# Moving the second layer's bias to ScalarE, running its last 64 features in pairs on two row tiles, and dropping PE's waits on itself

## The chip, the cores and the metric

The kernel runs on one core of a Trainium2 chip. The metric is the device time of one execution in microseconds (us). Each kernel was run four to six times, and the kernel before beside it; the ratios use runs in the fast state, and every profile shown fell in that state, with a granted TensorE clock of 1.0. Lines such as L735 are lines of the kernel's source. PE is TensorE's matmul, PEld its weight load, ACT is ScalarE, DVE is VectorE. PSUM holds the sums of the matmuls, here in eight banks; to evict a bank is to copy its result out. A matmul on a row tile uses 64 of the 128 rows of TensorE's array (shape 64\*128 in the profile), one on a column tile 64 of its 128 columns (128\*64).

## The reference, cut to what matters

```python
g = sigmoid((x * gate_w).sum(-1, keepdims=True))
a = A(x)        # a state-space model: B projection, recurrence over time, C projection
h = gelu(x @ w1 + b1)            # x: 2048 tokens x 640, w1: 640 x 1728
b = h @ w2 + b2                  # w2: 1728 x 640
out = g * a + (1 - g) * b
```

The inner width is 1728 = 13 x 128 + 64. A contraction over it takes 13 full slices of 128 rows and one of 64. This last, half-empty slice is what the change is about.

## The kernel before: the parts that matter

The kernel is a list of operations with priorities. A small scheduler in Python orders them for each engine, and each operation waits on the semaphores of the operations that it depends on:

```python
def run(eg, deps=deps, eng=eng, fn=fn):
    E.wait(eng, *[d.done for d in deps])        # also where PE depends on PE
    return fn()
```

The tokens are 16 chunks of 128. For each chunk the second layer makes two outputs of 128 x 320, one for each half of the 640 columns, each in a PSUM bank of its own. The banks rotate through all eight. The last slice has 64 features and, as row 65, a row of ones against which the weights hold the bias:

```python
def m2(c):                                       # second layer, chunk c
    q, t4 = c // 4, c % 4
    for hf in range(2):
        bank = next_bank()
        ...
        for jf in range(NF):                     # NF = 14 slices
            n = 128 if jf < NF - 1 else FL + 1   # the last: 64 features and the ones
            t = nc.tensor.matmul(PS[bank][:, 0:HALF],
                                 Gl[q % 2][0:n, jf, t4 * 128:(t4 + 1) * 128], W2sb[0:n, jf, cols],
                                 start=(jf == 0), stop=(jf == NF - 1))
        ...                                      # then ScalarE evicts the bank, times 1 - g

def outs(q):
    for c in range(4 * q, 4 * q + 4):
        m2(c); cproj(c); comb(c)                 # cproj: the C projection, 20 matmuls of 320 columns
```

The first layer has the same odd slice on its output side. It was already run as pairs, on two *column* tiles (`m1_tail`, two blocks of tokens at a time, 10 matmuls). This gives a model for what the change does.

Of the kernel before, what the change touches and what calls it, by code (L numbers as in the profile page):

```python
# [9 lines left out]
BF16 = mybir.dt.bfloat16  # L10
I32 = mybir.dt.int32
ACT = mybir.ActivationFunctionType
# [135 lines left out]
class Prog:  # L148
# [8 lines left out]
    def op(self, name, eng, dur, reads, writes, fn, prio=None, lat=0.0, after=()):  # L157
        deps = {}
        for k in reads:
            for w in self.last_w.get(k, ()):  # L160
                deps[w.idx] = w
        for k in writes:
            for w in self.last_w.get(k, ()):
                deps[w.idx] = w
            for r in self.last_r.get(k, ()):
                deps[r.idx] = r
        for a in after:
            deps[a.idx] = a
        deps = list(deps.values())
        E = self.E  # L170

        def run(eg, deps=deps, eng=eng, fn=fn):
            E.wait(eng, *[d.done for d in deps])
            return fn()

        it = self.sch.add(name, eng, dur, deps, run, prio=prio, lat=lat)
        for k in writes:
            self.last_w[k] = [it]
            self.last_r[k] = []
        for k in reads:  # L180
            self.last_r.setdefault(k, []).append(it)
        return it


def bass_gated_mix__ssm_conv_s5__dense_activation_gelu__prompt_kernel(
# [18 lines left out]
    _, S, D = A_x.shape  # L204
    P = A_Lambda_re.shape[0]
    F = B_w1.shape[1]
    assert S % 512 == 0 and D % 128 == 0 and P == D
    KD = D // 128
    KP = P // 128
    NQ = S // 512  # L210
    NCH = S // 128
    T = 256
    NB = S // T
    NF = (F + 127) // 128
    FL = F - (NF - 1) * 128
    assert FL <= 64
    HALF = D // 2
# [8 lines left out]
    with ExitStack() as es:  # L226

        def SB(name, shape, dt):
            return es.enter_context(nc.sbuf_tensor(name, list(shape), dt))

        xT = [SB(f"xT_{i}", [128, KD, 512], BF16) for i in range(NQ)]
        xn = [SB(f"xn_{i}", [128, 4, D], BF16) for i in range(2)]
        W1sb = SB("W1sb", [128, KD, F], BF16)
        W2sb = SB("W2sb", [128, NF, D], BF16)
        BT = SB("BT", [128, 2, KD, P], BF16)
        CT = SB("CT", [128, 2, KP, D], BF16)
        Gl = [SB(f"Gl_{i}", [128, NF, 512], BF16) for i in range(2)]
        dsk = SB("dsk", [128, D], BF16)
        gwb = SB("gwb", [128, D], BF16)
        rows = SB("rows", [128, 128], BF16)  # L240
        cols = SB("cols", [128, 3 * KP + NF], FP32)
        lcol = cols[:, 0:3 * KP].rearrange("p (a k) -> p a k", a=3)
        b1col = cols[:, 3 * KP:3 * KP + NF]
# [42 lines left out]
        PS = [es.enter_context(nc.psum_tensor(f"ps{i}", [128, 512], FP32)) for i in range(8)]  # L286
# [10 lines left out]
        E = Emitter(nc, engines, sems)  # L297
        E.count = dict.fromkeys(sems, 0)
        pr = Prog(E)
        op = pr.op  # L300

        def inc(eng, ins):
            return E.inc(eng, ins, eng + "_s")
# [8 lines left out]
        def d_act(n):  # L312
            return 0.26 + n * 0.00084
# [4 lines left out]
        def d_mm(n):  # L318
            return n / 2400.0 + 0.004


        def load(name, eng, sem, dst, src, writes, prio, dur=0.5, lat=2.5, reads=(), **kw):
            def fn():
                return dma_inc(eng, engines[eng].dma_start(dst, src), sem)
            return op(name, eng, dur, reads, writes, fn, prio=prio, lat=lat)
# [16 lines left out]
        nmain = (NF - 1) * 128  # L342
# [58 lines left out]

        op("warm", "pe", 3.2, ["wz"], [("bank", 6)], f_warm, prio=-1000)

        def f_ones():
            inc("dve", nc.vector.memset(Gl[0][64:65, NF - 1, :], 1.0))
            return inc("dve", nc.vector.memset(Gl[1][64:65, NF - 1, :], 1.0))

        op("ones", "dve", 1.1, (), ["gl1"], f_ones, prio=-40)

        XT = {q: [("xT", q, k) for k in range(KD)] for q in range(NQ)}  # L410

        psC = PS[7][:, :].bitcast(BF16)[:, 0:128]
# [140 lines left out]
        xnload(0, "sp", prio=32.4)  # L553
        load("w2a", "sp", "l_w2a", W2sb[:, 0:NF - 1, :], B_w2[0:nmain, :].rearrange("(j p) d -> p j d", p=128), ["w2a"], prio=33, lat=8.0)
        load("w2b", "sp", "l_w2b", W2sb[0:FL, NF - 1, :], B_w2[nmain:F, :], ["w2b"], prio=34, lat=4.0)
        for ci, src in enumerate((A_C_re, A_C_im)):
            load_T(f"C{ci}", f"l_C{ci}", [(CT[:, ci, :, :], src)], [("CT", ci)], prio=36 + ci, dur=4.1)
        load("dsk", "sp", "l_dsk", dsk[:, :], A_Dskip.partition_broadcast(128), ["dsk"], prio=38)
# [6 lines left out]
        def pe_prio():  # L565
            ctr["pe"] += 1
            return ctr["pe"]


        def next_bank():  # L570
            ctr["bank"] += 1
            return (ctr["bank"] - 1) % 8
# [21 lines left out]
        def m1_first():  # L594
            seq = [(k, jf) for k in range(KD) for jf in range(NW)]
            seq.remove((0, NW - 1))
            seq.insert(seq.index((1, NW - 1)), (0, NW - 1))
            for k, jf in seq:

                def f_mm(jf=jf, k=k):  # L600
                    return inc("pe", nc.tensor.matmul(PS[jf][:, :], W1sb[:, k, jf * 128:(jf + 1) * 128], xT[0][:, k, :],  # L601
                                                      start=(k == 0), stop=(k == KD - 1)))

                op(f"m1_0_{jf}_{k}", "pe", d_mm(512), [("xT", 0, k), ("w1", k)], [("bank", jf)] + (["late"] if (k, jf) == (KD - 1, 0) else []),
                   f_mm, prio=pe_prio())
            for jf in range(NW):
                ctr["bank"] += 1

                def f_ge(jf=jf):
                    return inc("act", nc.scalar.activation(Gl[0][:, jf, :], PS[jf][:, :], ACT.Gelu_apprx_tanh, bias=b1col[:, jf:jf + 1]))  # L610

                op(f"ge_0_{jf}", "act", d_act(512), [("bank", jf), "b1col"], [("gl", 0, jf)], f_ge, prio=10)
# [19 lines left out]
        def m1_tail(q):  # L632
            bank = next_bank()

            def f_mm():
                t = None
                for k in range(KD):
                    for i in range(2):
                        t = nc.tensor.matmul(PS[bank][64 * i:64 * i + FL, :], W1sb[:, k, nmain:F], xT[q + i][:, k, :],  # L639
                                             start=(k == 0), stop=(k == KD - 1))  # L640
                return inc("pe", t)

            op(f"m1t_{q}", "pe", KD * d_mm(512) + 0.25, XT[q] + XT[q + 1] + [("w1", "r")], [("bank", bank)], f_mm, prio=pe_prio())
            for i in range(2):

                def f_ge(i=i):
                    return inc("act", nc.scalar.activation(Gl[i][0:FL, NF - 1, :], PS[bank][64 * i:64 * i + FL, :], ACT.Gelu_apprx_tanh,
                                                           bias=b1col[64 * i:64 * i + FL, NF - 1:NF]))

                op(f"get_{q}_{i}", "act", d_act(512), [("bank", bank), "b1col"], [("gl", i, NF - 1)], f_ge, prio=10)  # L650

        def bproj(q):
            for ci in range(2):
# [68 lines left out]
            op(f"post{b}", "dve", 2 * d_dve(2560, 2) + 2 * d_dve(1280, 2), ["W", "ptab"], ["V", ("H", b % NHB)], f_post, prio=102 + 10 * b)  # L722


        def m2(c):
            q, t4 = c // 4, c % 4
            for hf in range(2):
                bank = next_bank()
                cols = slice(hf * HALF, (hf + 1) * HALF)

                def f_mm(bank=bank, cols=cols):
                    t = None
                    for jf in range(NF):
                        n = 128 if jf < NF - 1 else FL + 1
                        t = nc.tensor.matmul(PS[bank][:, 0:HALF], Gl[q % 2][0:n, jf, t4 * 128:(t4 + 1) * 128], W2sb[0:n, jf, cols],  # L735
                                             start=(jf == 0), stop=(jf == NF - 1))
                    return inc("pe", t)

                op(f"m2_{c}_{hf}", "pe", NF * d_mm(HALF), [("gl", q % 2, jf) for jf in range(NF)] + ["gl1", "w2a", "w2b", "b2"],
                   [("bank", bank)], f_mm, prio=pe_prio())  # L740

                def f_ev(bank=bank, cols=cols):
                    return inc("act", nc.scalar.activation(E1[c % NE][:, cols], PS[bank][:, 0:HALF], ACT.Copy, scale=g1col[:, c:c + 1]))  # L743

                op(f"e1_{c}_{hf}", "act", d_act(HALF), [("bank", bank), ("g", q)], [("E1", c % NE, hf)], f_ev, prio=5)


        cbank = {}

# [66 lines left out]

            op(f"st{c}", "sp", 0.5, [("osb", c % NO, 0), ("osb", c % NO, 1)], [], f_st, prio=1000 + c, lat=2.5)

        def outs(q):
            for c in range(4 * q, 4 * q + 4):  # L820
                m2(c)
                cproj(c)
                comb(c)

        m1_first()
        load("b2", "pool", "l_b2", W2sb[64:65, NF - 1, :], B_b2.rearrange("(o n) -> o n", o=1), ["b2"], prio=-30, dur=1.0, reads=["late"])

        m1(0, NW)
        bproj(0)
        ssm(0)  # L830
        gates(0)
        m1(1)
        m1_tail(0)
        ssm(1)
        bproj(1)
        ssm(2)
        gates(1)
        outs(0)
        for q in range(2, NQ):
            ssm(2 * q - 1)  # L840
            bproj(q)
            ssm(2 * q)
            m1(q)
            if q % 2 == 1:
                m1_tail(q - 1)
            xnload(q, "pool")
            gates(q)
            outs(q - 1)
        ssm(2 * NQ - 1)
        outs(NQ - 1)  # L850

        order = pr.sch.order()
        ptr = {e: 0 for e in order}
# [57 lines left out]
```

## Time and profile before

| | before |
|---|---|
| time, median of 3 (later 4) runs | 216.51 us |
| span of the profiled execution | 215.1 us |
| PE / DVE / ACT busy | 98% / 88% / 46% |
| second-layer matmuls | 448, of which 32 have 65 rows |

The busy line of the page (engine, busy us, share of the span, number of instruction records; POOL is GpSimd):

```profile
PE 210.9 (98%) x1247; PEld 122.0 (57%) x1257; DVE 189.3 (88%) x262; ACT 99.0 (46%) x169; POOL 3.0 (1%) x11
```

The chain of work that ended last, in order of time (start us, length us, what); L735 is the second layer, L762 the C projection, L639 the first layer's tail, L660 the B projection, and "issue" is time in which the engine waited for nothing that the profile shows:

```profile
45.30 1.22 PE ps L639 x10
46.52 0.14 issue
46.66 10.74 PE ps L660 x49
57.40 3.81 PE ps L735 x28
61.21 2.72 PE ps L762 x20
63.93 3.81 PE ps L735 x28
67.74 2.72 PE ps L762 x20
...
```

TensorE is the limit, and it does not stop: 28 matmuls of 320 columns take 3.81 us, 136 ns each, and the next group follows at once. In such a stream only a change in the number or the spacing of matmuls moves the time.

The groups by shape (line, engine, operation, out<-in, shapes, count, then busy us and mean ns, then idle before):

```profile
L735 PE MATMUL ps<-W2sb,Gl 128*128 128x320 bf16 x416 | 61.4, 299 | 0.0
L735 PE MATMUL ps<-W2sb,Gl 65*128 65x320 bf16 x32 | 9.6, 301 | 0.0
L639 PE MATMUL ps<-xT,W1sb 128*64 128x512 bf16 x20 | 2.5, 384 | 0.0
...
L743 ACT ACTIVATE E<-ps,g1col 128x320 bf16<-128x320 f32 x32 | 16.9, 527 | 43.8 <-PE ps L735 43.8
L647 ACT ACTIVATE Gl<-ps,cols 64x512 bf16<-64x512 f32 x4 | 2.7, 683 | 1.1 <-PE ps L639 1.0
```

A matmul of 65 rows lasts as long as one of 128 (301 and 299 ns; these are latencies, and the next one starts 136 ns later). The 20 tail matmuls of L639 are busy for 2.5 us in all, because they run two at a time.

### The profile page before, as it was taken

The numbers are of one execution on the slowest core, as the hardware profiler recorded it, in microseconds if no ns is written. First come the engines' busy times: TensorE is split into PE (matmuls) and PEld (weight loads), VectorE is DVE, ScalarE is ACT, GpSimd is POOL, SyncE is SP. The second block draws the span as 40 slices with busy tenths as digits, with TensorE's granted clock in tenths as the row PEclk, the third lists the DMA queues.
The fourth block names the chain that finished last, engine by engine and source line by source line (L and its number), as shares of the span: only waits on it lengthen the run. The fifth ranks groups of instructions, "written<-read, shape, count | busy, mean of one in ns | idle before, by whom it ended". The sixth has DMA issues, their size and how long they took to land.

```text
span 215.1 us, 3184 instructions
## 1 busy us (share of the span) xinstructions
PE 210.9 (98%) x1247; PEld 122.0 (57%) x1257; DVE 189.3 (88%) x262; ACT 99.0 (46%) x169; POOL 3.0 (1%) x11
## 2 busy tenths in 40 slices
PE   7999999999999999999999999999999999999995
PEld 2344444444577775444467777444447777777773
DVE  3599999999999999999999999699999999959512
ACT  2469556675432224556642332556664233233220
POOL 1010000000000100000000010000000000000000
PEclk9999999999999999999999999999999999999999
DMA  6999799994000230100000022000000000000001
GB/s 132 293 274 200 196 382 227 215 216 101 0 0 34 43 140 0 34 0 0 3 0 30 0 84 103 30 3 0 0 0 3 8 35 21 30 30 30 34 30 30
DMA packets 30681, 16.09 MB, mean 75 GB/s; under 512 B 23948, under 2 KB 29772, under 8 KB 30668
## 3 DMA queue, kind: packets, MB, share of 16 engines
q1 hardware_dynamic: 30144, 14.32, 27.1%
q0 software_dynamic: 320, 1.31, 2.0%
q10 hardware_dynamic: 204, 0.27, 0.5%
q8 instruction: 10, 0.16, 0.3%
q14 instruction: 3, 0.02, 0.0%
HBM read 7.38 MB, written 2.62 MB: 47 GB/s over the span
## 4 chain that ended last, share of the span: by engine, by line
PE 98%; DVE 0%; issue 0%
PE ps L735 28%; PE ps L621 22%; PE ps L762 20%; PE ps L660 20%; PE ps L601 5%; PE ps L399 2%; PE ps L639 1%; DVE osb L795 0%; DVE wz L392 0%; PE ps L415 0%
## 5 line engine op out<-in xcount | busy, mean ns | idle before, releaser
L735 PE MATMUL ps<-W2sb,Gl 128*128 128x320 bf16 x448 | 63.6, 299 | 0.0
L735 PEld LDWEIGHTS ps<-W2sb,Gl 128*128 128x128 bf16 x448 | 43.8, 98 | 17.5
L621 PE MATMUL ps<-xT,W1sb 128*128 128x512 bf16 x214 | 47.3, 379 | 0.3
L762 PE MATMUL ps<-CT,H 128*128 128x320 bf16 x320 | 46.2, 299 | 0.0
L700 DVE TENSOR_TENSOR_SCAN W<-atab,V 128x1280 bf16<-128x1280 f32 x16 | 44.3, 2811 | 0.3
L660 PE MATMUL ps<-xT,BT 128*128 128x512 bf16 x196 | 43.1, 379 | 0.3 <-PE ps L639 0.2
L762 PEld LDWEIGHTS ps<-CT,H 128*128 128x128 bf16 x320 | 31.2, 98 | 12.6 <-issue 0.4
L743 ACT ACTIVATE E<-ps,g1col 128x320 bf16<-128x320 f32 x32 | 16.9, 527 | 43.8 <-PE ps L735 43.8
L628 ACT ACTIVATE Gl<-ps,cols 128x512 bf16<-128x512 f32 x44 | 29.8, 694 | 15.5 <-PE ps L621 15.5
L621 PEld LDWEIGHTS ps<-xT,W1sb 128*128 128x128 bf16 x220 | 21.5, 98 | 26.0
L660 PEld LDWEIGHTS ps<-xT,BT 128*128 128x128 bf16 x200 | 19.5, 98 | 23.5 <-issue 0.4
L669 ACT ACTIVATE U<-ps 128x512 bf16<-128x512 f32 x40 | 23.9, 597 | 18.3 <-PE ps L660 18.3
L773 ACT ACTIVATE E<-ps,gcol 128x320 bf16<-128x320 f32 x30 | 15.8, 527 | 24.2 <-PE ps L762 24.1
L465 DVE TENSOR_TENSOR osb<-xg,E 128x640 bf16<-128x640 bf16 x15 | 7.3, 486 | 9.0 <-ACT E L773 8.0
L781 DVE SCALAR_TENSOR_TENSOR xg<-xn,gcol,dsk 128x640 bf16<-128x640 bf16 x16 | 13.9, 883 | 0.4
L578 DVE SCALAR_TENSOR_TENSOR scr<-xn,gwb 128x640 bf16<-128x640 bf16 x16 | 13.2, 823 | 0.4
L465 DVE TENSOR_TENSOR V<-V,W 128x1280 bf16<-128x1280 bf16 x16 | 12.5, 821 | 0.3
L465 DVE TENSOR_TENSOR H<-H,V 128x1280 bf16<-128x1280 bf16 x16 | 12.5, 821 | 0.3
L465 DVE TENSOR_TENSOR V<-mr,U 128x2560 bf16<-128x2560 bf16 x8 | 11.9, 1489 | 0.2
L465 DVE TENSOR_TENSOR H<-c,W 128x2560 bf16<-128x2560 bf16 x8 | 11.9, 1490 | 0.1
L465 DVE TENSOR_TENSOR V<-s,W 128x2560 bf16<-128x2560 bf16 x8 | 11.9, 1485 | 0.0
L465 DVE TENSOR_TENSOR W<-mi,U 128x2560 bf16<-128x2560 bf16 x8 | 11.9, 1484 | 0.0
(77 smaller groups left out, 84.7 us busy)
## 6 DMA issues: line engine op xcount, KB each, us to landing
out_dram<-osb SPq DMA_DIRECT2D x15, 160.0 KB, 1.8
W2sb<-in_B_w_dram SPq DMA_DIRECT2D x1, 2080.0 KB, 11.1
xn<-in_A_x_dram SPq DMA_DIRECT2D x2, 640.0 KB, 6.0
xn<-in_A_x_dram POOLq DMA_DIRECT2D x2, 640.0 KB, 4.8
W1sb<-in_B_w_dram SPq DMA_DIRECT2D x4, 256.0 KB, 4.2
W1sb<-in_B_w_dram SPq DMA_DIRECT2D x1, 880.0 KB, 6.1
W1sb<-in_B_w_dram ACTq DMA_DIRECT2D x1, 256.0 KB, 2.7
gwb<-in_gate_w_dram SPq DMA_DIRECT2D x1, 160.0 KB, 5.6
```

What stands on the lines that cost most here:

```text
L465: return inc("dve", nc.vector.tensor_tensor(out=o, in0=a, in1=b, op=o_))
L578: t = inc("dve", nc.vector.scalar_tensor_tensor(out=scr[:, :], in0=xn[q % 2][:, c, :], scalar=1.0, in1=gwb[:, :], op0=ALU.mult, op1=ALU.mu ...
L621: t = nc.tensor.matmul(PS[bank][:, :], W1sb[:, k, jf * 128:(jf + 1) * 128], xT[q][:, k, :], start=(k == 0), stop=(k == KD - 1))
L628: return inc("act", nc.scalar.activation(Gl[q % 2][:, jf, :], PS[bank][:, :], ACT.Gelu_apprx_tanh, bias=b1col[:, jf:jf + 1]))
L660: t = nc.tensor.matmul(PS[bank][:, :], BT[:, ci, kd, k * 128:(k + 1) * 128], xT[q][:, kd, :], start=(kd == 0), stop=(kd == KD - 1))
L669: return inc("act", nc.scalar.activation(dst, src, ACT.Copy, scale=1.0 if ci == 0 else -1.0))
L700: t = inc("dve", nc.vector.tensor_tensor_scan(out=g[:, ci, :], data0=a, data1=v[:, ci, :], initial=0.0, op0=ALU.mult, op1=ALU.add))
L735: t = nc.tensor.matmul(PS[bank][:, 0:HALF], Gl[q % 2][0:n, jf, t4 * 128:(t4 + 1) * 128], W2sb[0:n, jf, cols], start=(jf == 0), stop=(jf == ...
L743: return inc("act", nc.scalar.activation(E1[c % NE][:, cols], PS[bank][:, 0:HALF], ACT.Copy, scale=g1col[:, c:c + 1]))
L762: t = nc.tensor.matmul(PS[bank][:, 0:HALF], H[b % NHB][:, ci, k, s * 128:(s + 1) * 128], CT[:, ci, k, cols], start=(i == 0), stop=(i == 2 ...
L773: return inc("act", nc.scalar.activation(E2[c % NE][:, cols], PS[bank][:, 0:HALF], ACT.Copy, scale=gcol[:, c:c + 1]))
L781: return inc("dve", nc.vector.scalar_tensor_tensor(out=xg[c % 2][:, :], in0=xn[q % 2][:, c % 4, :], scalar=gcol[:, c:c + 1], in1=dsk[:, :] ...
```

## The change

The intent: if the bias is put in PSUM beforehand, the last slice has 64 rows and fits half of the array. The two halves of a chunk then use the two row tiles side by side, in two banks, and 32 matmuls become 16 pairs. Pairs of two or three chunks are run together, because entering and leaving the tiled mode costs something. A bank's sum is now made in separate pieces: the tails of a whole group run right after the full slices of its first chunk, and for the other chunks they add to the bias before the full slices do. The old waits would hold each piece back until the one before it on the bank was complete, so PE's waits on itself are dropped too.

Four parts matter (cut):

```diff
-            E.wait(eng, *[d.done for d in deps])
+            E.wait(eng, *[d.done for d in deps if not (eng == "pe" and d.eng == "pe")])
...
+        def m2_prime(c):                      # ScalarE writes the bias into both banks
+            ...
+                    return inc("act", nc.scalar.activation(PS[bank][:, 0:HALF], b2b[:, cols], ACT.Copy))
...
-                    for jf in range(NF):
-                        n = 128 if jf < NF - 1 else FL + 1
-                        t = nc.tensor.matmul(..., start=(jf == 0), stop=(jf == NF - 1))
+                    for jf in range(NF - 1):
+                        t = nc.tensor.matmul(..., start=False, stop=False, skip_group_check=True)
...
+        def m2_tails(cs):
+            def f_mm():
+                for c in cs:
+                    q, t4 = c // 4, c % 4
+                    for hf in range(2):
+                        r = slice(64 * hf, 64 * hf + FL)     # rows 0-63 or 64-127
+                        t = nc.tensor.matmul(PS[mbank[c, hf]][:, 0:HALF],
+                                             Gl[q % 2][r, NF - 1, t4 * 128:(t4 + 1) * 128],
+                                             W2sb[r, NF - 1, hf * HALF:(hf + 1) * HALF],
+                                             start=False, stop=False, skip_group_check=True)
...
-        def outs(q):
-            for c in range(4 * q, 4 * q + 4):
-                m2(c)
+        def outs(*cs):
+            for c in cs:
+                m2_prime(c)
+            for c in cs:
+                m2_main(c)
+                if c == cs[0]:
+                    m2_tails(cs)
+                m2_out(c)
                 cproj(c)
                 comb(c)
```

The chunks are taken as (0,1), (2,3), (4,5), (6,7), (8,9,10), (11,12,13), (14,15): seven groups. The tail GELU is made twice, into rows 0-63 and 64-127. The last rows of `w2` are loaded twice, and `b2` is loaded broadcast to all partitions. The memset of the ones goes.

Accumulating onto what ScalarE wrote is not a matter of course. The Trainium skill, "PSUM — Partial Sum Buffer", The four PSUM rules, says that a matmul without the start flag adds where the bank's written bit is set, that a matmul sets this bit, and that ScalarE's writes leave it alone. Here every bank has been written by matmuls over these columns before its bias is.

More of the change, by code (lines that the diff above doesn't have):

```diff
@@ L239, in bass_gated_mix__ssm_conv_s5__dense_activation_gelu__prompt_kernel @@
         gwb = SB("gwb", [128, D], BF16)
+        b2b = SB("b2b", [128, D], BF16)
         rows = SB("rows", [128, 128], BF16)
@@ L402, in bass_gated_mix__ssm_conv_s5__dense_activation_gelu__prompt_kernel @@
         op("warm", "pe", 3.2, ["wz"], [("bank", 6)], f_warm, prio=-1000)
-        def f_ones():
-            inc("dve", nc.vector.memset(Gl[0][64:65, NF - 1, :], 1.0))
-            return inc("dve", nc.vector.memset(Gl[1][64:65, NF - 1, :], 1.0))
-        op("ones", "dve", 1.1, (), ["gl1"], f_ones, prio=-40)
         XT = {q: [("xT", q, k) for k in range(KD)] for q in range(NQ)}
@@ L555, in bass_gated_mix__ssm_conv_s5__dense_activation_gelu__prompt_kernel @@
         load("w2b", "sp", "l_w2b", W2sb[0:FL, NF - 1, :], B_w2[nmain:F, :], ["w2b"], prio=34, lat=4.0)
+        load("w2c", "sp", "l_w2c", W2sb[64:64 + FL, NF - 1, :], B_w2[nmain:F, :], ["w2c"], prio=34.2, lat=4.0)
+        load("b2", "sp", "l_b2", b2b[:, :], B_b2.partition_broadcast(128), ["b2"], prio=34.4)
         for ci, src in enumerate((A_C_re, A_C_im)):
@@ L602, in f_mm @@
                                                       start=(k == 0), stop=(k == KD - 1)))
-                op(f"m1_0_{jf}_{k}", "pe", d_mm(512), [("xT", 0, k), ("w1", k)], [("bank", jf)] + (["late"] if (k, jf) == (KD - 1, 0) else []),
+                op(f"m1_0_{jf}_{k}", "pe", d_mm(512), [("xT", 0, k), ("w1", k)], [("bank", jf)] ,
                    f_mm, prio=pe_prio())
@@ L644, in m1_tail, with f_ge @@
             for i in range(2):
-                def f_ge(i=i):
-                    return inc("act", nc.scalar.activation(Gl[i][0:FL, NF - 1, :], PS[bank][64 * i:64 * i + FL, :], ACT.Gelu_apprx_tanh,
-                                                           bias=b1col[64 * i:64 * i + FL, NF - 1:NF]))
-                op(f"get_{q}_{i}", "act", d_act(512), [("bank", bank), "b1col"], [("gl", i, NF - 1)], f_ge, prio=10)
+                for u in range(2):
+                    def f_ge(i=i, u=u):
+                        return inc("act", nc.scalar.activation(Gl[i][64 * u:64 * u + FL, NF - 1, :], PS[bank][64 * i:64 * i + FL, :], ACT.Gelu_apprx_tanh,
+                                                               bias=b1col[64 * i:64 * i + FL, NF - 1:NF]))
+                    op(f"get_{q}_{i}{u}", "act", d_act(512), [("bank", bank), "b1col"], [("gt", i, u)], f_ge, prio=10)
         def bproj(q):
@@ L722, in ssm, with f_pr, m2_main @@
             op(f"post{b}", "dve", 2 * d_dve(2560, 2) + 2 * d_dve(1280, 2), ["W", "ptab"], ["V", ("H", b % NHB)], f_post, prio=102 + 10 * b)
-        def m2(c):
+        mbank = {}
+        def m2_prime(c):
+            for hf in range(2):
+                bank = next_bank()
+                mbank[c, hf] = bank
+                cols = slice(hf * HALF, (hf + 1) * HALF)
+                def f_pr(bank=bank, cols=cols):
+                    return inc("act", nc.scalar.activation(PS[bank][:, 0:HALF], b2b[:, cols], ACT.Copy))
+                op(f"pr_{c}_{hf}", "act", d_act(HALF), ["b2"], [("bank", bank)], f_pr, prio=8)
+        def m2_main(c):
             q, t4 = c // 4, c % 4
             for hf in range(2):
-                bank = next_bank()
+                bank = mbank[c, hf]
                 cols = slice(hf * HALF, (hf + 1) * HALF)
@@ L732, in f_mm, with m2_out @@
                     t = None
-                    for jf in range(NF):
-                        n = 128 if jf < NF - 1 else FL + 1
-                        t = nc.tensor.matmul(PS[bank][:, 0:HALF], Gl[q % 2][0:n, jf, t4 * 128:(t4 + 1) * 128], W2sb[0:n, jf, cols],
-                                             start=(jf == 0), stop=(jf == NF - 1))
+                    for jf in range(NF - 1):
+                        t = nc.tensor.matmul(PS[bank][:, 0:HALF], Gl[q % 2][:, jf, t4 * 128:(t4 + 1) * 128], W2sb[:, jf, cols],
+                                             start=False, stop=False, skip_group_check=True)
                     return inc("pe", t)
-                op(f"m2_{c}_{hf}", "pe", NF * d_mm(HALF), [("gl", q % 2, jf) for jf in range(NF)] + ["gl1", "w2a", "w2b", "b2"],
+                op(f"m2_{c}_{hf}", "pe", (NF - 1) * d_mm(HALF), [("gl", q % 2, jf) for jf in range(NF - 1)] + ["w2a"],
                    [("bank", bank)], f_mm, prio=pe_prio())
+        def m2_tails(cs):
+            def f_mm():
+                t = None
+                for c in cs:
+                    q, t4 = c // 4, c % 4
+                    for hf in range(2):
+                        r = slice(64 * hf, 64 * hf + FL)
+                        t = nc.tensor.matmul(PS[mbank[c, hf]][:, 0:HALF], Gl[q % 2][r, NF - 1, t4 * 128:(t4 + 1) * 128],
+                                             W2sb[r, NF - 1, hf * HALF:(hf + 1) * HALF], start=False, stop=False, skip_group_check=True)
+                return inc("pe", t)
+            op(f"m2t_{cs[0]}", "pe", len(cs) * d_mm(HALF) + 0.2, [("gt", c // 4 % 2, u) for c in cs for u in range(2)] + ["w2b", "w2c"],
+               [("bank", mbank[c, hf]) for c in cs for hf in range(2)], f_mm, prio=pe_prio())
+        def m2_out(c):
+            q = c // 4
+            for hf in range(2):
+                bank = mbank[c, hf]
+                cols = slice(hf * HALF, (hf + 1) * HALF)
                 def f_ev(bank=bank, cols=cols):
@@ L825, in bass_gated_mix__ssm_conv_s5__dense_activation_gelu__prompt_kernel @@
         m1_first()
-        load("b2", "pool", "l_b2", W2sb[64:65, NF - 1, :], B_b2.rearrange("(o n) -> o n", o=1), ["b2"], prio=-30, dur=1.0, reads=["late"])
         m1(0, NW)
@@ L837, in bass_gated_mix__ssm_conv_s5__dense_activation_gelu__prompt_kernel @@
         gates(1)
-        outs(0)
+        outs(0, 1)
+        outs(2, 3)
         for q in range(2, NQ):
@@ L847, in bass_gated_mix__ssm_conv_s5__dense_activation_gelu__prompt_kernel @@
             gates(q)
-            outs(q - 1)
+            if q < NQ - 1:
+                outs(4 * q - 4, 4 * q - 3)
+                outs(4 * q - 2, 4 * q - 1)
+        outs(NCH - 8, NCH - 7, NCH - 6)
         ssm(2 * NQ - 1)
-        outs(NQ - 1)
+        outs(NCH - 5, NCH - 4, NCH - 3)
+        outs(NCH - 2, NCH - 1)
         order = pr.sch.order()
```

## The prediction

> **What bounds the kernel now.** TensorE: PE is busy 98% of the 215.1 us span (the page's busy table) and is 98% of the chain of waits that ended last. In order of time it is one unbroken stream: 28 second-layer matmuls of 320 columns take 3.81 us (136 ns each), 49 of 512 columns 10.75 us. VectorE is busy 88%, ScalarE 46%.
>
> **What the change removes.** Of 448 second-layer matmuls, 32 carry the last 64 features plus a row of ones for the bias (65 rows) and cost as much as full ones: 32 x 136 ns = 4.35 us of the critical stream. Without the bias they have 64 rows and run as 16 pairs on two row tiles. In the first layer's tail (column tiles) the trace shows the matmuls of a pair starting 4 ns apart and pairs 216 ns apart: a pair costs one matmul. If row tiles do the same, 16 pairs cost 2.2 us: gross gain 2.15 us.
>
> **What it adds on PE.** The pairs sit between full-array matmuls in 7 groups (2,2,2,2,3,3,2 pairs): 7 entries to and 7 exits from the tiled mode. "TensorEngine Tiling (Array Packing)", Key Properties, in the Trainium skill says that changing the mode drains TensorE. The trace agrees: entering the first layer's tail, start to start is 309 ns in place of 216 (+93), and its first pair takes 240 (+24); leaving it, where no wait on PE follows, +95 and +12. Estimate: the sum, 0.22 us a group, 1.55 us in all.
>
> **Self-waits.** Dropping PE's waits on itself is needed as slices now share banks in flight. Before, it costs once: after the first tail the successor waits on PE, +322 ns in place of +95: 0.2 us.
>
> **Off the critical path.** ScalarE gets 32 bias writes of 128x320 into PSUM. Estimate from the 512-column copy (597 ns), less 192 columns at the 0.833 ns that the skill's "ScalarE: Activation LUTs", Step-by-step, states: 0.44 us each, 14 us; plus four tail GELUs at 0.68 us: busy 116 us. A bank for the next group's bias comes free at least one slice of 2.7 us ahead, against 1 us of eviction and bias write. I expect no stall of PE. Two extra loads (80 and 160 KB) delay the transposes of C by perhaps 1 us; those are issued by 39 us, used from 61 us. H of the last block is ready at 200.2 us, used at 203.6.
>
> **Sum.** 216.5 - 2.15 + 1.55 - 0.2 = 215.7 us. Range 214.7 to 216.7. Faster by over 2%: 0.02; within 2%: 0.95; slower by over 2%: 0.03.
>
> **What would show it.** 32 matmuls of 64x128; starts in a pair a few ns apart; a group of two pairs taking 0.49 us between the full matmuls (0.27 matmul, 0.22 switching). Chain of waits: still PE 98%. ScalarE busy 114 to 118 us, the bias write 0.40 to 0.48 us. No PE idle time released by ScalarE.
>
> **What would make it wrong.** (1) Row tiles don't overlap as column tiles do, perhaps because two weight loads (98 ns each) don't hide under 136 ns: pairs save nothing, switches cost, 217 us or more. (2) Switching by rows is cheaper than by columns: down to 214.2. (3) The static order puts a bias write behind a late eviction in ScalarE's queue, or the last scan's output behind late additions in VectorE's: PE waits a few us.

## The result and the profile after

| | time, median | range | ratio to before, fast runs | 95% interval |
|---|---|---|---|---|
| before | 216.51 us | 216.29 to 216.86 | | |
| after | 215.17 us | 215.07 to 215.31 | 0.9937 | 0.992 to 0.9954 |
| before, the same rounds as the repeat | 216.13 us | 215.98 to 217.04 | | |
| after, repeated later | 215.10 us | 214.94 to 215.59 | 0.9954 | 0.9941 to 0.9966 |

The ratios are from the fast runs of the same rounds; they are not quite the ratios of the medians in the table, nor always those of plain means. The gain is 1.34 us by the first pair of medians and 1.03 us by the second: real, and within 2%. The outputs are right.

The busy line of after:

```profile
PE 210.0 (98%) x1257; PEld 119.3 (56%) x1257; DVE 188.3 (88%) x260; ACT 112.9 (53%) x205; POOL 2.5 (1%) x10
```

The chain of after, the same stretch (L745: full slices of the second layer, L759: the pairs, L791: the C projection, L636: the first layer's tail):

```profile
44.89 1.20 PE ps L636 x10
46.09 10.90 PE ps L658 x50
56.99 3.53 PE ps L745 x26
60.52 0.38 PE ps L759 x4
60.90 2.82 PE ps L791 x20
63.72 3.53 PE ps L745 x26
67.25 2.72 PE ps L791 x20
69.97 3.53 PE ps L745 x26
...
```

In the chain a piece starts where the one before it ends, so latencies shift its borders by a little; the sums are what counts. A chunk's second layer went from 3.81 to 3.53 us. The four tail matmuls of two chunks cost 0.38 us in a block of their own, and the C projection after the block takes 2.82 us in place of 2.72. So 2 x 3.81 = 7.62 us became 2 x 3.53 + 0.38 + 0.10 = 7.54 us. That is the whole gain from a group of two pairs, and it is small.

The groups by shape of after, PE and then ACT:

```profile
L745 PE MATMUL ps<-W2sb,Gl 128*128 128x320 bf16 x416 | 59.1, 299 | 0.0
L759 PE MATMUL ps<-W2sb,Gl 64*128 64x320 bf16 x32 | 3.4, 301 | 0.0
...
L773 ACT ACTIVATE E<-ps,g1col 128x320 bf16<-128x320 f32 x32 | 16.1, 526 | 42.2 <-PE ps L759 18.3 <-PE ps L745 17.5 <-DVE g1col L587 5.1
L732 ACT ACTIVATE ps<-b2b 128x320 f32<-128x320 bf16 x32 | 14.0, 440 | 0.9
L645 ACT ACTIVATE Gl<-ps,cols 64x512 bf16<-64x512 f32 x8 | 5.5, 683 | 1.2 <-PE ps L636 1.0
```

The bias write takes 440 ns. "ScalarE: Activation LUTs", What ACT_TABLE_LOAD costs, gives 186 ns + 0.833 ns per element for an activation without pointer operands, an estimate of 453 ns for 320: the trace agrees within 3%.

The timeline of the weight loads around one group (start us, length us, engine, line, what, count, idle before):

```profile
60.45 0.12 PEld L759 LDWEIGHTS ps<-W2sb,Gl 64*128 64x128 bf16 x4 [0.26 <-issue]
60.83 0.11 PEld L791 LDWEIGHTS ps<-CT,H 128*128 128x128 bf16 x2 [0.26 <-issue]
```

In the plain stream a weight load starts with the matmul before its own, some 135 ns ahead. At the entry to the group and at the exit the loader sits idle for 0.26 us, and its load then starts only 4 to 5 ns ahead of its own matmul. Record by record, the trace has these starts around the group (the times here are 5 ns below the views' scale; the differences are what counts):

```
60.216  full slice (last of chunk 0)
60.448  pair 1, rows 0-63       +232 ns   (96 more than 136)
60.451  pair 1, rows 64-127       +3
60.594  pair 2, rows 0-63       +143      (from the row above)
60.598  pair 2, rows 64-127       +4
60.826  C projection, first     +228      (92 more than 136)
60.972  C projection, second    +146      (10 more)
```

All seven groups show the same +96 and +92 within 1 ns, so the switch is a constant. "TensorEngine Tiling (Array Packing)", Key Properties, says that changing the tiling mode drains TensorE. The trace agrees that TensorE pauses, and supplies the price that the page lacks. The pause is shorter than a wait for completion: the first pair starts 232 ns after the last full matmul, before that one's modelled end at 299 ns, and b_after_waits below shows 359 ns where PE does wait for it. "TensorE: Matmul & The Clock Gate", Part 3, Measured speedup vs the span model, lets each further tile of a pack add about 4 ns; here the matmuls of a pair start 3 and 4 ns apart, and 2 to 4 ns over all seven groups.

### Splitting the run so that the start's noise drops out

To compare the kernels to better than 0.1 us, I cut each trace at three matmuls, all taken from the records. The *restart* is the first matmul after the small transpose of the parameter rows, at some 7.5 us. The *second part* begins at the first matmul of 320 columns, at some 57 us. The end is the start of the last matmul.

| kernel | restart | restart to second part | second part | restart to end |
|---|---|---|---|---|
| before | 7.57 | 49.669 | 155.273 | 204.942 |
| before, repeated | 7.99 | 49.669 | 155.272 | 204.941 |
| after | 7.39 | 49.434 | 154.446 | 203.880 |
| after, repeated | 7.40 | 49.435 | 154.446 | 203.881 |

From the restart on, two traces of one kernel agree within 2 ns. What varied between them by more than some 10 ns lay before it. What the change gained after the restart is therefore 204.942 - 203.880 = 1.06 us: 0.235 us in the first part and 0.827 us in the second. The two measured gains (1.34 and 1.03 us) fit this plus the noise of the start, which varied by 0.4 us between the two traces of before.

### The profile page after: what moved, and what is told of

Read it like the earlier page. It is cut to its first block, busy times and chain, and to the rows that moved or that the text cites. A ratio compares the mean times of both kernels' runs of the same rounds, so it can differ in the third digit from the quotient of the medians.

```text
span 213.8 us, 3098 instructions
## 1 busy us (share of the span) xinstructions
PE 210.0 (98%) x1257; PEld 119.3 (56%) x1257; DVE 188.3 (88%) x260; ACT 112.9 (53%) x205; POOL 2.5 (1%) x10
## 4 chain that ended last, share of the span: by engine, by line
PE 95%; DMA 2%; SPq 1%; DVE 0%; issue 0%
PE ps L745 26%; PE ps L618 22%; PE ps L791 21%; PE ps L658 20%; PE ps L598 3%; DMA W1sb<-in_B_w_dram 2%; PE ps L759 1%; SPq L332 1%; PE ps L636 1%; DVE osb L824 0%
## 5 line engine op out<-in xcount | busy, mean ns | idle before, releaser
L745 PE MATMUL ps<-W2sb,Gl 128*128 128x320 bf16 x416 | 59.1, 299 | 0.0
L745 PEld LDWEIGHTS ps<-W2sb,Gl 128*128 128x128 bf16 x416 | 40.6, 98 | 16.5 <-ACT Gl L625 0.4
L618 PE MATMUL ps<-xT,W1sb 128*128 128x512 bf16 x220 | 48.1, 379 | 0.0
L791 PE MATMUL ps<-CT,H 128*128 128x320 bf16 x320 | 46.1, 299 | 0.0
L658 PE MATMUL ps<-xT,BT 128*128 128x512 bf16 x200 | 43.8, 379 | 0.0
L773 ACT ACTIVATE E<-ps,g1col 128x320 bf16<-128x320 f32 x32 | 16.1, 526 | 42.2 <-PE ps L759 18.3
L791 PEld LDWEIGHTS ps<-CT,H 128*128 128x128 bf16 x320 | 30.7, 98 | 13.5 <-issue 1.8
L732 ACT ACTIVATE ps<-b2b 128x320 f32<-128x320 bf16 x32 | 14.0, 440 | 0.9
```

Of the source, the lines that this page charges most:

```text
L618: t = nc.tensor.matmul(PS[bank][:, :], W1sb[:, k, jf * 128:(jf + 1) * 128], xT[q][:, k, :], start=(k == 0), stop=(k == KD - 1))
L658: t = nc.tensor.matmul(PS[bank][:, :], BT[:, ci, kd, k * 128:(k + 1) * 128], xT[q][:, kd, :], start=(kd == 0), stop=(kd == KD - 1))
L732: return inc("act", nc.scalar.activation(PS[bank][:, 0:HALF], b2b[:, cols], ACT.Copy))
L745: t = nc.tensor.matmul(PS[bank][:, 0:HALF], Gl[q % 2][:, jf, t4 * 128:(t4 + 1) * 128], W2sb[:, jf, cols], start=False, stop=False, skip_gr ...
L773: return inc("act", nc.scalar.activation(E1[c % NE][:, cols], PS[bank][:, 0:HALF], ACT.Copy, scale=g1col[:, c:c + 1]))
L791: t = nc.tensor.matmul(PS[bank][:, 0:HALF], H[b % NHB][:, ci, k, s * 128:(s + 1) * 128], CT[:, ci, k, cols], start=(i == 0), stop=(i == 2 ...
```

## The experiments

The theory after seeing both traces: (1) the pairs save what they should, and seven switches of 0.21 us take most of it back; (2) one self-wait of PE in the first layer accounts for the 0.235 us; (3) the remaining 0.14 us are a small extra cost of the 65-row shape; (4) ScalarE's new work costs nothing. The rivals stand in the expectations.

### a_before_nowait: the kernel before, without PE's waits on itself

```diff
 # before.py
-            E.wait(eng, *[d.done for d in deps])
+            E.wait(eng, *[d.done for d in deps if not (eng == "pe" and d.eng == "pe")])
```

> The kernel before with the one line that drops PE's waits on itself, nothing else. Theory T1: of the 1.34 us that the change gained, 0.22 us come from a single self-wait in the first layer (at 9.1 us the eighth slice's second matmul follows its first on the same bank; start to start 440 ns in place of 216), and little else: 216.3 us, and in the trace that gap is gone. Rival T2 (the prediction's place): the self-wait costs 0.2 us at the exit of the first layer's tail (46.1 us); then the exit gap shrinks by 0.2 us and the one at 9.1 us stays. Rival T3: the self-waits explain the whole surplus over the pairs, some 0.6 us: 215.9 us.

Measured: 216.20 us against 216.21 us, ratio 0.9996 (0.998 to 1.0013). Restart to second part 49.435 us, second part 155.271 us. So T1 holds in the trace: 0.234 us are gone from the first part, nothing from the second. T3 falls, because the self-waits do not explain the second part. The time of the whole run does not resolve 0.23 us; the gain is shown by the trace alone.

The weight loads of before near 9 us, and those of this kernel at the same place:

```profile
8.87 0.10 PEld L601 LDWEIGHTS ps<-xT,W1sb 128*128 128x128 bf16 x1
9.52 0.33 PEld L601 LDWEIGHTS ps<-xT,W1sb 128*128 128x128 bf16 x3 [0.55 <-PE ps L601]
```

```profile
8.73 0.96 PEld L601 LDWEIGHTS ps<-xT,W1sb 128*128 128x128 bf16 x5
```

The "<-PE" marks a wait for PE. In the kernel before, the eighth slice's second matmul follows its first directly on the same bank, and waits until the first is complete: 440 ns start to start in place of 216. Every kernel here with self-waits has this gap (439 or 440 ns); none without them has it.

### h_before_again: the kernel before once more

> The kernel before, unchanged, for a second trace of it. The start up to the first second-layer matmul varied by 0.6 us among the kernels that share it. If the self-wait is what the new start saves, the 440 ns gap at the eighth slice is here again, and the first second-layer matmul starts later than 57.1 us; if that gap was chance, it is not here. Ratio to before 1.000 within 0.2%, which is the noise of the method.

Measured: 216.29 us, ratio 1.0012 (0.9998 to 1.0025). The 439 ns gap is there again. The first 320-column matmul starts at 57.66 us, later than 57.1 as expected, but that sign was a poor one: k_before_full below has the self-wait too and starts it at 56.76 us, because the start varies. This trace also settles T2, the place that the prediction named. First the exit of the first layer's tail in the old trace, then in the new one (timeline of PE):

```profile
46.66 0.59 PE L660 MATMUL ps<-xT,BT 128*128 128x512 bf16 x2 [0.16 <-PE ps L639]
```

```profile
46.54 0.38 PE L639 MATMUL ps<-xT,W1sb 128*64 128x512 bf16 x2
46.86 0.61 PE L660 MATMUL ps<-xT,BT 128*128 128x512 bf16 x2
```

In the new trace the exit costs +95 ns, like the exit at the other tail and like the exits of after; nothing waits there. The new trace has 1257 matmul records for 1257 weight loads, the old one 1247. The +322 ns that I had read as a self-wait were one lost record: the old trace's step of 538 ns is the new one's 311 and 227 ns in one.

### b_after_waits: the kernel after, with the self-waits put back

```diff
 # after.py
-            E.wait(eng, *[d.done for d in deps if not (eng == "pe" and d.eng == "pe")])
+            E.wait(eng, *[d.done for d in deps])
```

> The kernel after with PE's waits on itself put back. If the wait on the own semaphore adds to the drain at a group's entry (the tails write the banks that the slice just before them wrote), the entry grows from 232 ns start to start by 100 to 150 ns in 7 groups, plus 0.22 us in the first layer: 1.0 to 1.3 us more than after, about 216.3 us. Rival: the mode switch drains the array anyway, so only the 0.22 us of the first layer come back: 215.4 us.

Measured: 216.86 us, ratio 1.0021 (1.0003 to 1.0038), slower than the kernel before by 0.2%. Restart to end is 205.302 us, 1.42 us more than after, where 1.0 to 1.3 were expected: 0.234 in the first part, 1.188 in the second. The waits of the weight loader in the second part, of this kernel and of after (who waited for whom: us in total, times, longest):

```profile
PEld ps L759 <- PE ps L745: 2.0, 5, 0.4
PEld ps L791 <- issue: 1.8, 7, 0.3
PEld ps L759 <- issue: 1.0, 2, 0.6
...
```

```profile
PEld ps L791 <- issue: 1.8, 7, 0.3
PEld ps L759 <- issue: 1.8, 7, 0.3
...
```

The tails now wait for the slice just before them, by this view at five of the seven entries. These five take 359 ns in place of 232, so the wait adds 127 ns to the drain. Two entries, at 60.6 and 164.2 us, take 559 and 449 ns; what adds the further 200 and 90 ns there stays open (the view shows nothing that they wait for). The rival (the drain hides the wait) falls. The one-line filter is worth 1.42 us in the new kernel, more than the whole change gained; in the old kernel it is worth 0.23.

### d_full: no pairs, no switches, everything else of the change kept

```diff
 # after.py
-        load("w2c", "sp", "l_w2c", W2sb[64:64 + FL, NF - 1, :], B_w2[nmain:F, :], ["w2c"], ...)
+        (GpSimd sets W2sb[64:128, NF - 1, :] to zero)
...
-                        r = slice(64 * hf, 64 * hf + FL)
+                        r = slice(0, 128)
```

> The kernel after with the last slices as full 128-row matmuls (upper 64 rows of the weights zero), same order and bias writes by ScalarE: no pairs and no mode switch. Theory: 32 x 136 ns come in, 16 pairs and 7 switches go out, so 0.69 us slower than after: 215.85 us; that is the kernel before less its self-waits. Rival (the pairs hardly gain and the bias by ScalarE is the gain, since the slices of 65 rows cost more than full ones): within 0.2 us of after.

Measured: 215.96 us, ratio 0.9983 (0.9968 to 0.9999). The second part takes 155.132 us. Against after (154.446) this is +0.686 us: what pairs and switches are worth together, as expected. Against before (155.273) it is -0.141 us: bias writes, new order, dropped self-waits and full rows together cost nothing there and even gain a little.

### k_before_full: is the 0.14 us the shape?

```diff
 # before.py: the last slice with 128 rows, ones against zero weights
-            inc("dve", nc.vector.memset(Gl[0][64:65, NF - 1, :], 1.0))
+            inc("dve", nc.vector.memset(Gl[0][64:128, NF - 1, :], 1.0))     # and Gl[1]
...
+        (GpSimd sets W2sb[64:128, NF - 1, :] to zero before the bias is loaded into row 64)
...
-                        n = 128 if jf < NF - 1 else FL + 1
+                        n = 128
```

> The kernel before with the last slice's 65 rows filled up to 128 (ones against zero weights; same result, same order, same waits, bias still in the matmul). The stretch from the first to the last 320-column matmul starts took 155.27 us before, 155.27 without self-waits, and 155.13 with full slices and ScalarE's bias. Theory: the 0.14 us are the 65-row shape (the trace shows 140 and 139 ns, then 135, around each such matmul), so the stretch becomes 155.13 us here too. Rival: they come from the bias or the order, and the stretch stays 155.27 us. The time of the whole run changes by too little to tell.

Measured: 216.10 us, ratio 0.9998 (0.9986 to 1.0011). The second part takes 155.131 us, and the first 49.669, self-wait included. The theory holds: in the kernel before, the two steps after the start of each 65-row matmul are 140 and 138 to 139 ns and then 135 again, and filled up to 128 rows the slices lose the same 0.14 us as in d_full. Zeros in the idle rows were cheaper than leaving the rows out. And since d_full, with the bias by ScalarE, the new order and no self-waits, agrees with this kernel within 1 ns in the second part, those three together cost or gain nothing there.

### e_onerow: both matmuls of a pair on one row tile

```diff
 # after.py
-                        r = slice(64 * hf, 64 * hf + FL)
+                        r = slice(0, FL)
```

> The kernel after with both matmuls of a pair on the same row tile (rows 0 to 63), same groups, same switches, same result. Theory: the matmuls of a pair no longer overlap, 16 more times 136 ns: 2.17 us more than after, 217.3 us, and starts in a pair 136 ns apart in place of 4. Rival (two row tiles don't overlap in fact and the trace's starts are only modelled): same time as after.

Measured: 217.49 us against 216.37 us, ratio 1.0053 (1.0037 to 1.007). The second part takes 156.599 us, 2.153 us more than after; expected were 2.17. Its group of L759 and the chain at its first block:

```profile
L759 PE MATMUL ps<-W2sb,Gl 64*128 64x320 bf16 x32 | 5.5, 298 | 0.0
```

```profile
60.78 0.65 PE ps L759 x4
61.42 2.82 PE ps L791 x20
...
```

The same four matmuls with the same switches take 0.65 us in place of 0.38. The overlap of the row tiles is real, and it is worth the full 2.15 us that the prediction called the gross gain. The switches are in both kernels, so they must be priced by another experiment.

### c_singles: sixteen groups of one pair

```diff
 # after.py
                 m2_main(c)
-                if c == cs[0]:
-                    m2_tails(cs)
+                m2_tails([c])
```

> The kernel after with 16 groups of one pair instead of 7 groups of two or three pairs, same pairs, same bias writes. If what eats the gain is a fixed cost per entry and exit, 0.20 us as the trace of after shows (610 ns from the last full matmul to the next one for two pairs, less two pairs and one full matmul of 136 ns), 9 more groups cost 1.8 us: 217.0 us, slower than before. Rival (the cost is per pair, not per switch): unchanged, 215.2 us.

Measured: 217.46 us, ratio 1.0053 (1.0037 to 1.0069). The second part takes 156.358 us, 1.912 us more than after for nine more groups: 0.212 us a group. The chain at its first two groups:

```profile
60.77 0.24 PE ps L759 x2
61.02 2.82 PE ps L791 x20
63.84 3.53 PE ps L745 x26
67.37 0.24 PE ps L759 x2
67.61 2.82 PE ps L791 x20
...
```

Two matmuls now need 0.24 us of the block and another 0.10 us after it. One pair saves one matmul of 136 ns and pays a switch of 212 ns: a group of one pair is a loss. The rival (a cost per pair) falls. The total was 0.5 us above my number; 0.11 of this is the slope (1.91 and not 1.8). The restart of its trace was also 0.25 us later than that of after (7.64 us).

### f_prime2: every bias write twice

```diff
 # after.py, in m2_prime
                 def f_pr(bank=bank, cols=cols):
+                    E.wait("act", inc("act", nc.scalar.activation(PS[bank][:, 0:HALF], b2b[:, cols], ACT.Copy)))
                     return inc("act", nc.scalar.activation(PS[bank][:, 0:HALF], b2b[:, cols], ACT.Copy))
```

> The kernel after with every bias write made twice, the second waiting for the first: ScalarE busy 113 to about 127 us. Theory: ScalarE's bias writes are off the critical path, within 0.2 us of after (215.2 us), no wait of PE on ScalarE. Rival: they delay PE a little now, and twice as many would cost 0.5 us or more.

Measured: 215.49 us against 216.37 us, ratio 0.9952 (0.9936 to 0.9968), ScalarE busy 125.3 us. The whole-run median is 0.3 us above that of after, outside the 0.2 us expected; the traces, free of the start, say less. The second part takes 154.558 us, 0.112 us more than after, all of it in one place. The view of the weight loader's waits from 100 us on names it (L760 is the pairs here, L645 the tail GELU; the view's other lines go with no longer step between matmuls than in after):

```profile
PEld ps L760 <- ACT Gl L645: 0.4, 1, 0.4
```

At the group of chunks 8 to 10, which comes right after the first layer's last tail, the pairs waited for the tail GELU: the entry took 345 ns and not 232. So the expected "no wait of PE on ScalarE" did not hold, but the rival's 0.5 us did not come either. ScalarE's writes are off the critical path in after; twice as many of them use up the margin at one of seven groups.

### g_four and h_four_again: four groups of four pairs

If a switch costs 0.212 us and a pair saves 0.136, larger groups should win. All eight banks can be given the bias of four chunks, if the C projection runs one chunk behind, into banks just evicted:

```diff
 # after.py
-            for c in cs:
+            for i, c in enumerate(cs):
                 m2_main(c)
-                if c == cs[0]:
+                if i == 0:
                     m2_tails(cs)
                 m2_out(c)
-                cproj(c)
-                comb(c)
+                if i > 0:
+                    cproj(cs[i - 1])
+                    comb(cs[i - 1])
+            cproj(cs[-1])
+            comb(cs[-1])
...            # and outs() is called with 4 chunks at a time, four times
```

> A version meant to beat both: 4 groups of four pairs. All eight banks take the bias of four chunks, the product with C runs one chunk behind. Theory: three groups fewer at 0.20 us each: 0.6 us less than after, 214.6 us. Rival: eight banks held at once leave ScalarE too little time between the last eviction of the stage before and the tails, PE waits at each group's start, and the gain is lost or reversed (215.2 us or more).

> The version with four groups of four pairs, again, beside the kernel after on the same chip: 0.6 us faster than it, stretch of the second part 153.81 us. Rival: its earlier margin was the start's noise, then the two agree within 0.2 us.

> The kernel after, unchanged, beside the four-pair version on the same chip: 215.2 us; stretch of the second part 154.45 us as before.

Measured: 214.58 us, ratio 0.9919 (0.9905 to 0.9932). Repeated beside the kernel after on the same chip: 214.25 us, ratio 0.9914 (0.9898 to 0.9929), while after had 215.10 us, ratio 0.9954 (0.9941 to 0.9966). The intervals do not overlap, so it beats both kernels, if by less than 2%. The medians of the repeat differ by 0.85 us and not by the expected 0.6; the traces give the expected size. The second part takes 153.809 and 153.811 us, 0.637 us less than after: 0.212 us for each of the three groups saved, the same price as in c_singles. Its first group in the chain:

```profile
56.83 3.53 PE ps L745 x26
60.36 0.65 PE ps L759 x8
61.01 5.40 PE ps L745 x39
...
```

Eight matmuls in 0.65 us. All four entries are 231 or 232 ns, the same as in after: PE loses no time to ScalarE at any of them, and the rival falls.

## Why the prediction was right

The time lies in the range: 215.17 us measured (215.10 on repeat), 215.7 predicted, 214.7 to 216.7 allowed, and the forecast was "within 2%". The gain was 1.06 us from the restart on, predicted were 0.8. The range was wider than the gain, and an unchanged kernel (216.5 us) would have fallen into it too, so the total alone says little; the parts say more. Point by point:

- **What bounds the kernel: right.** PE stayed at 98% busy, and each experiment that moved the matmul stream moved the second part by the same amount.
- **Gross gain 2.15 us: right.** Taking the overlap away cost 2.153 us (e_onerow). The column tiles of the first layer's tail were a good model for the row tiles.
- **Seven switches at 0.22 us, 1.55 us: right, slightly too high.** The slope over 16, 7 and 4 groups is 0.212 us a group both ways, 1.48 us for seven. Net of pairs and switches, 0.686 us was measured (d_full) and 0.60 predicted.
- **Self-waits, 0.2 us: right in size, wrong in the reason.** I put it at the exit of the first layer's tail, where the record of a matmul was missing from the trace. A real self-wait of 0.235 us stood elsewhere, in the first layer at 9.1 us. That the two agree is luck. A count of records (1247 matmuls for 1257 weight loads) would have warned me.
- **Missed: the 65-row shape, 0.14 us.** The prediction let these matmuls cost as much as full ones. Only k_before_full showed that this comes from the shape and not from the bias.
- **Missed: the worth of the dropped self-waits in the new kernel.** The prediction called dropping them needed, but put no number on it; keeping them would have cost 1.42 us and turned the gain into a loss (b_after_waits).
- **ScalarE: right in effect, slightly high in size.** The bias write took 440 ns, as estimated. Busy time rose to 112.9 us, below the stated 114 to 118; part of the difference is overlap of neighbouring instructions (the 32 evictions of the second layer were busy for 16.1 us in place of 16.9, at 526 and 527 ns each). No lost time of PE came of it. The two transposes of C started 1.9 and 1.3 us later (mean of two traces of each kernel), where perhaps 1 us was predicted, and no cost of it shows. f_prime2 shows the margin to be thin at one group.
- **The stated signs came**: matmuls of a pair 2 to 4 ns apart, and a group of two pairs costing 0.48 us (0.38 in the block, 0.10 after it) where 0.49 was predicted.

The sum of the parts closes: 0.235 (self-wait) + 0.141 (shape) + 0.686 (pairs less switches) = 1.06 us. The rest of the 1.34 us between the first two medians, 0.28 us, is within the noise of the start: in the traces of all kernels here the restart lay between 7.03 and 7.99 us, and the repeat of after beside before gave 1.03 us.

## What to carry to other kernels

Packing two half-height matmuls saves one matmul, and each visit to the tiled mode costs a fixed price that can be read off an existing visit. Here 212 ns against 136 ns saved by a pair made one pair a loss, two a small gain and four a good one, so first ask how many pairs the PSUM banks allow per visit. When accumulation in one bank is split into separate pieces, look for waits of an engine on itself: they cost 1.42 us here, more than the 0.69 us that the packing gave. Before reading a gap as a wait, count the records, and cut the trace where the noise ends: the whole-run times could not resolve what the trace gave to 2 ns.

## What the Trainium skill lacked or had wrong

- "TensorEngine Tiling (Array Packing)" says that changing the mode drains TensorE, but gives no price. Between matmuls of 320 columns a round trip from 128-row to 64-row tiles cost 0.212 us, whether 3 or 9 round trips were taken away or added. The same kind of step was +93 and +95 ns for the column tiles of the first layer's tail.
- No page has it that the weight load is not pulled ahead over such a switch. The loader sat idle 0.26 us at each entry and exit, and the load started 4 to 5 ns before its own matmul, in place of some 135 ns.
- No page has the price of a wait of PE on its own last matmul: 439 ns in place of 216 between two matmuls of 512 columns on one bank, and 127 ns on top of the drain at a switch.
- "TensorE: Matmul & The Clock Gate" (Why this matters for your kernels) says that a single matmul with a contraction of 32 rows takes the same time as one with 128. The runs had 65 rows, and there it was nearly but not quite so: the two steps after a 65-row matmul starts took 140 and 138 to 139 ns in place of 136 each, and 32 such matmuls cost 0.14 us more than with their rows filled up to 128. Matmuls of 64 rows on one row tile (e_onerow) were 136 ns apart, as the page has it.
